# A 1x1 depthwise-separable convolution: pw loaded two thirds once and one third four times, transposes in thirds

**Chip, cores, metric.** One NeuronCore of a Trainium2 chip. The metric is the device time of one execution in microseconds (us), lower is better. Runs of a kernel are compared with runs of the kernel before on the same chip in the same rounds. A profile shows one of these executions, as the hardware profiler took it; its span is about 1.7 us shorter than the run time of the same execution.

## The reference

```python
H = W = 384; C = 384; k = 1
x: (1, H, W, C) bf16    dw: (1, 1, C) bf16    pw: (C, C) bf16
out = x * dw[0, 0]                     # k = 1: one factor for each channel
return einsum('bhwc,cd->bhwd', out, pw)
```

So out = x (147,456 rows of 384) times the matrix diag(dw) pw. x comes in and the result goes out once, 113 MB each way.

## The kernel before

x is cut into 288 supertiles of 512 rows. VectorE transposes 4-byte words, each word a pair of bf16 channels (uint32 in the profile, 876 ns for 128x384 of them). TensorE's stationary operand `T[.., par::2]` has 32 rows of channels of one parity (32*128 in the profile), and four matmuls run side by side, one in each strip of 32 array rows (`tile_position`): one takes 321 ns, yet four are done every 162.6 ns. The kernel gives each strip the scaled weights on the strip's own 32 partitions. The head of the kernel makes this fourfold, channel-sorted copy `w_r`: TensorE multiplies pw by a selection matrix `sel_w` that holds dw, and ScalarE and VectorE copy the results out of PSUM.

```python
nc.scalar.dma_start(dw_row[:], ...).then_inc(s_dw, 16)
load_x(0, nc.scalar)                                   # first x chunk: ScalarE's queue
nc.sync.dma_start(pw_n[:], pw.rearrange("(k p) d -> p k d", p=P)).then_inc(s_pw, 16)
...                                                    # then x chunks 1, 2, ... on nc.sync
w_eng = [1, 0, 1, 1, 1, 1]                             # who copies block i: 1 ScalarE, 0 VectorE
w_first = {(0, 0): [(0, 1), (1, 3)], (4, 0): [(1, 4)], (4, 1): [(1, 5)]}
...
nc.tensor.wait_ge(s_zero, 1); idle_work(3)             # 12 matmuls of zeros, in all four strips
...                                                    # dw to columns, 3 small matmuls
idle_work(3)                                           # 12 more
nc.tensor.wait_ge(s_pw, 16)
times = {(1, 1): 3, (2, 0): 2}                         # some copies repeated: 18 matmuls of 64 rows
for k in range(3): ...                                 # copies of pw to the four quadrants
with nc.tensor.Fori(0, NS // 2, 1) as it: ...          # the stream: 48 matmuls a supertile
...
for h in range(2):                                     # two transposes a supertile, 128x384 words
    ins = nc.vector.transpose(out=Tw[:, 3*h : 3*h+3], in_=Xw[:, :, j, 96*h : 96*h+96]...)
```

Of the kernel before, what the change touches and what calls it, by code (L numbers as in the profile page):

```python
# [7 lines left out]
BF16 = mybir.dt.bfloat16  # L8
F32 = mybir.dt.float32
U32 = mybir.dt.uint32  # L10
COPY = mybir.ActivationFunctionType.Copy
# [16 lines left out]
def kernel(  # L28
# [12 lines left out]
    nc = tc.nc  # L41
    P = nc.NUM_PARTITIONS
    B, H, W, C = x.shape
    assert dw.shape[0] == 1 and dw.shape[1] == 1, "only k=1 depthwise supported"
    D = pw.shape[1]
# [22 lines left out]
    pw_n = consts.tile([P, 3, D], BF16, name="pw_n")  # L68
    ones = consts.tile([P, P], BF16, name="ones")
    eye = consts.tile([P, P], BF16, name="eye")  # L70
    sel = consts.tile([P, 2, 32], F32, name="sel")
    sel_w = consts.tile([P, 3, 2, 4, 32], BF16, name="sel_w")
    w_r = consts.tile([P, NB, 2, D], BF16, name="w_r")
    dw_row = consts.tile([1, C], BF16, name="dw_row")
    dw_f = consts.tile([P, 3], F32, name="dw_f")
# [6 lines left out]
    Os = [bufp.tile([P, 4 * LMAX * D], BF16, name=f"O{i}") for i in range(NR)]  # L82
    PS = [psum.tile([P, 4, 512], F32, name=f"ps{s}") for s in range(2)]
# [3 lines left out]
    s_t = [[nc.alloc_semaphore(f"s_t{i}{h}") for h in range(2)] for i in range(2)]  # L87
# [5 lines left out]
    s_pw = nc.alloc_semaphore("s_pw")  # L93
    s_df = nc.alloc_semaphore("s_df")
    s_sw = nc.alloc_semaphore("s_sw")
    s_dwf = nc.alloc_semaphore("s_dwf")
    s_sel = nc.alloc_semaphore("s_sel")
    s_w = nc.alloc_semaphore("s_w")
    s_wr = [nc.alloc_semaphore(f"s_wr{e}") for e in range(2)]
# [3 lines left out]
    with tc.tile_critical():  # L103
# [8 lines left out]
        def load_x(t, eng=nc.sync):  # L112
            g, i, off, first, L = chunks[t]
            dst, sem, _ = x_of(t)
            rows = xf[512 * first : 512 * (first + L), :]
            if first + LONG < NS:
                src = rows.rearrange("(p s) c -> p (s c)", p=P)
                dst = dst.rearrange("p s c -> p (s c)")
                if i == 0 and g >= NR:
                    je = g_end[g - NR]  # L120
                    eng.wait_ge(s_t[je % 2][1], je // 2 + 1)
            else:
                src = rows.rearrange("(a k q) c -> q a k c", k=4, q=4)
            eng.dma_start(dst, src).then_inc(sem, 16)
# [16 lines left out]

        nc.scalar.dma_start(dw_row[:], dw.rearrange("a e c -> a (e c)")).then_inc(s_dw, 16)
        load_x(0, nc.scalar)
        nc.sync.dma_start(pw_n[:], pw.rearrange("(k p) d -> p k d", p=P)).then_inc(s_pw, 16)

# [5 lines left out]
        for _, f, t in sorted(todo, key=lambda a: a[0]):  # L151
            if f is store and t == 0:

                for _ in range(28):
                    nc.sync.wait_ge(s_pw, 16)
            f(t)
# [7 lines left out]
        w_eng = [1, 0, 1, 1, 1, 1]  # L164
        w_done = [(s_wr[e], w_eng[: i + 1].count(e)) for i, e in enumerate(w_eng)]

        w_first = {(0, 0): [(0, 1), (1, 3)], (4, 0): [(1, 4)], (4, 1): [(1, 5)]}

        def w_ps(i):
            return PS[0 if i in (2, 3) else 1][:, 2 * (i % 2) : 2 * (i % 2) + 2, :D]  # L170


        steps = [(b, par) for b in range(4) for par in range(2)] + [(4, 0), (5, 0), (4, 1), (5, 1)]

        def supertile(s, rv):
            for b, par in steps:
                for q in range(4):
                    if q == 0 and par == 0 and b in (0, 3):
                        nc.tensor.wait_ge(s_t[s][b // 3], rv)
                    if q == 0 and s == 0:  # L180
                        for e, v in w_first.get((b, par), []):
                            nc.tensor.wait_ge(s_wr[e], v)
                    mm = nc.tensor.matmul(  # L183
                        PS[s][:, q, :D],
                        lhsT=Ts[s][32 * q : 32 * q + 32, b, par::2],
                        rhs=w_r[32 * q : 32 * q + 32, b, par, :],
                        start=(b, par) == steps[0],
                        stop=(b, par) == steps[-1],
                        tile_position=(32 * q, 0),
                    )  # L190
                    if (b, par) == steps[0] and q == 0:
                        mm._wait_ge(s_a[s], rv)
                    if (b, par) in ((2, 1), (5, 1)) and q == 3:
                        mm.then_inc(s_pe)


        def idle_work(n):
            with nc.tensor.Fori(0, n, 1) as _:
                for i in range(4):
                    nc.tensor.matmul(  # L200
                        PS[0][:, i, :D],
                        lhsT=zero[32 * i : 32 * i + 32, 0:P],
                        rhs=zero[32 * i : 32 * i + 32, :],
                        start=True,
                        stop=True,
                        tile_position=(32 * i, 0),
                    )

        nc.tensor.wait_ge(s_zero, 1)
        idle_work(3)  # L210
# [3 lines left out]
        for k in range(3):  # L214
            mm = nc.tensor.matmul(  # L215
                PS[1][:, 0, D + k : D + k + 1],
                lhsT=dw_row[:, P * k : P * k + P],
                rhs=ones[0:1, 0:1],
                start=True,
                stop=True,  # L220
            )
        mm.then_inc(s_df)
        idle_work(3)
        nc.tensor.wait_ge(s_pw, 16)
        times = {(1, 1): 3, (2, 0): 2}
        for k in range(3):
            nc.tensor.wait_ge(s_sw, k + 1)
            for r in range(2):
                if k == 2:
                    nc.tensor.wait_ge(*w_done[r])  # L230

                for v in [0, 1] * times.get((k, r), 1):
                    mm = nc.tensor.matmul(  # L233
                        PS[(k + 1) % 2][:, 2 * r + v, :D],
                        lhsT=sel_w[64 * v : 64 * v + 64, k, r, :, :].rearrange("p q w -> p (q w)"),
                        rhs=pw_n[64 * v : 64 * v + 64, k, :],
                        start=True,
                        stop=True,
                        tile_position=(64 * v, 0),
                    )  # L240
                mm.then_inc(s_w)
# [5 lines left out]

        nc.gpsimd.memset(warm[:], 0.0).then_inc(s_seed)  # L248
        nc.gpsimd.memset(zero[:].bitcast(U32), 0).then_inc(s_zero)  # L249
# [9 lines left out]
        )._wait_ge(s_seed, 2).then_inc(s_sel)  # L259
        for s in range(2):  # L260
            c = nc.scalar.copy(warm[:, s + 1 : s + 2], warm[:, 0:1])  # L261
            if s == 0:
                c._wait_ge(s_seed, 1)
            c.then_inc(s_a[s])

        def transposes(t, j):
            g, i, off, first, L = chunks[t]
            jj = first + j
            s = jj % 2
            X, sem, n = x_of(t)  # L270
            Xw = X.bitcast(U32).rearrange("p (k l) c -> p k l c", l=L)
            Tw = Ts[s][:].bitcast(U32).rearrange("p b (i k) -> p b k i", k=4)
            for h in range(2):
                if h == 0 and j == 0:
                    nc.vector.wait_ge(sem, n)
                ins = nc.vector.transpose(  # L276
                    out=Tw[:, 3 * h : 3 * h + 3],
                    in_=Xw[:, :, j, 96 * h : 96 * h + 96].rearrange("p k (b w) -> p b k w", w=32),
                )
                if jj >= 2:  # L280
                    ins._wait_ge(s_pe, 2 * (jj - 2) + h + 1)
                ins.then_inc(s_t[s][h])
# [3 lines left out]
        def w_out(i):  # L286
            e, k, r = w_eng[i], i // 2, i % 2
            out, in_ = w_r[:, 2 * k : 2 * k + 2, r, :], w_ps(i)
            o = nc.vector.tensor_copy(out, in_) if e == 0 else nc.scalar.copy(out, in_)  # L289
            o._wait_ge(s_w, i + 1)  # L290
            o.then_inc(s_wr[e])
# [4 lines left out]
            in_=eye[:].rearrange("p (v w r) -> p r w v", v=2, r=2),  # L296
# [4 lines left out]
        nc.vector.tensor_copy(dw_f[:], PS[1][:, 0, D : D + 3]).then_inc(s_dwf)  # L301
        nc.vector.wait_ge(s_dwf, 2)
        for k in range(3):
            nc.vector.tensor_scalar_mul(  # L304
                sel_w[:, k], sel[:].unsqueeze(2).to_broadcast([P, 2, 4, 32]), dw_f[:, k : k + 1]
            ).then_inc(s_sw)
        for i in range(6):
            w_out(i)
# [3 lines left out]
        for jj, (t, j) in enumerate(order):  # L312
# [6 lines left out]
            if jj + 1 == NS:  # L319
                nq = 2  # L320
                nc.vector.wait_ge(s_o[g % NR], 16 * sum(map(len, groups[g % NR : g : NR])))
                e = nc.vector.tensor_copy(Ov[:, nq:4, j, :], PS[s][:, nq:4, :D])  # L322
                e._wait_ge(s_pe, 2 * jj + 2)
                e.then_inc(s_d)
            a = nc.scalar.copy(Ov[:, 0:nq, j, :], PS[s][:, 0:nq, :D])  # L325
            a._wait_ge(s_pe, 2 * jj + 2)
# [36 lines left out]
```

## Time and profile before

| | kernel before |
|---|---|
| time, 4 runs | 575.41 us (575.3 to 575.55) |
| span of the profile | 573.4 us |
| head, to the first stream matmul | 6.84 us |
| stream, 288 supertiles | 561.80 us |
| busy: TensorE, VectorE, ScalarE | 99%, 88%, 73% |

Read it as a head, a stream in which TensorE never waits, and a tail. The chain, the groups and the head in order of time are shown and read in the prediction.

The granted clock doesn't tell that TensorE runs at half clock at first: that shows in the durations of matmuls (494 ns on average for the zero matmuls of this head and up to 524 for the copies, against 321 in the stream). "Half clock" below means matmuls that long; the changed kernel's profile has four of them start to start in 320 ns, against 162.5 at full clock.

### The profile page before, as it was taken

Reading aid. Unit: us, or ns where it says so; the run is one execution under the profiler, and the core shown is the slowest. Engines: PE = TensorE matmul, PEld = TensorE weight load, DVE = VectorE, ACT = ScalarE, POOL = GpSimd, SP = SyncE. Lnnn points to the kernel's source line nnn. Section 1 sums busy time; section 2 is a strip of 40 time slices with the busy share of each in tenths; the row PEclk is TensorE's granted clock in tenths of the full one; section 3 lists DMA queues with packets and bytes.
Section 4 is the critical chain, followed back from the end, with each engine's and each line's share of the span. In section 5 each row is a group of like instructions: output and inputs, shape, how many; then the busy total and the mean of one; then the engine's idle time right before and its main releaser. Section 6 shows DMA issues by size and latency. Waiting matters only on the chain.

```text
span 573.4 us, 29717 instructions
## 1 busy us (share of the span) xinstructions
PE 566.5 (99%) x13869; PEld 414.7 (72%) x13869; DVE 506.7 (88%) x583; ACT 419.0 (73%) x296; POOL 0.9 (0%) x8
## 2 busy tenths in 40 slices
PE   8999999999999999999999999999999999999996
PEld 5777777777777777777777777777777777777774
DVE  7898889889889888988988988898898898889884
ACT  6777777777777777777777777777777777777775
POOL 0000000000000000000000000000000000000000
PEclk9999999999999999999999999999999999999999
DMA  9999999999999999999999999999999999998676
GB/s 363 420 340 434 417 425 432 445 414 422 428 414 425 387 400 427 392 408 390 430 392 385 404 425 401 396 416 421 399 392 411 418 387 393 422 401 364 267 288 233
DMA packets 25253, 226.88 MB, mean 396 GB/s; under 512 B 1178, under 2 KB 5147, under 8 KB 21403
## 3 DMA queue, kind: packets, MB, share of 16 engines
q1 hardware_dynamic: 24064, 225.61, 97.0%
q10 hardware_dynamic: 1178, 1.18, 0.6%
q14 instruction: 10, 0.07, 0.0%
q8 instruction: 1, 0.02, 0.0%
HBM read 113.54 MB, written 113.25 MB: 396 GB/s over the span
## 4 chain that ended last, share of the span: by engine, by line
PE 99%; ACT 0%; DVE 0%; issue 0%; POOL 0%; POOLq 0%; SPq 0%
PE ps L183 98%; PE ps L200 0%; ACT w_r L289 0%; DVE O L322 0%; PE ps L233 0%; POOL zero L249 0%; POOL warm L248 0%; PE ps L215 0%; POOLq L358 0%; SPq L103 0%
## 5 line engine op out<-in xcount | busy, mean ns | idle before, releaser
L183 PE MATMUL ps<-w_r,T 32*128 32x384 bf16 x13824 | 561.8, 321 | 0.7 <-ACT w_r L289 0.7
L276 DVE STREAM_TRANSPOSE T<-X 128x384 uint32<-128x384 uint32 x572 | 500.0, 876 | 56.0 <-DMA X<-in_x_dram 0.3
L325 ACT CAST O<-ps 128x1536 bf16<-128x1536 f32 x288 | 413.8, 1437 | 147.6 <-PE ps L183 147.6
L183 PEld LDWEIGHTS ps<-w_r,T 32*128 32x128 bf16 x13824 | 412.9, 93 | 149.4 <-issue 0.9
L289 ACT CAST w_r<-ps 128x768 bf16<-128x768 f32 x5 | 3.6, 818 | 1.0 <-PE ps L233 1.0
L200 PE MATMUL ps<-zero 32*128 32x384 bf16 x24 | 2.6, 494 | 1.4 <-POOL zero L249 1.4
L276 DVE STREAM_TRANSPOSE T<-Xl 128x384 uint32<-128x384 uint32 x4 | 3.5, 876 | 0.4
L322 DVE CAST O<-ps 128x768 bf16<-128x768 f32 x1 | 1.0, 958 | 3.0 <-PE ps L183 3.0
L261 ACT ACT_TABLE_LOAD x1 | 1.3, 1283 | 1.9 <-issue 1.9
L200 PEld LDWEIGHTS ps<-zero 32*128 32x128 bf16 x24 | 0.7, 99 | 2.6 <-issue 2.6
L233 PE MATMUL ps<-pw_n,sel_w 64*128 64x384 bf16 x18 | 2.2, 403 | 0.0
L233 PEld LDWEIGHTS ps<-pw_n,sel_w 64*128 64x128 bf16 x18 | 1.0, 114 | 1.3 <-issue 0.7
L294 DVE TENSOR_REDUCE sel<-eye 128x64 f32<-128x128 bf16 x1 | 0.3, 290 | 1.8 <-POOL eye L251 1.8
L289 DVE CAST w_r<-ps 128x768 bf16<-128x768 f32 x1 | 1.0, 958 | 0.9 <-PE ps L233 0.9
L304 DVE TENSOR_SCALAR sel_w<-sel,dw_f 128x256 bf16<-128x256 f32 x3 | 0.9, 350 | 0.0
L301 DVE COPY dw_f<-ps 128x3 f32<-128x3 f32 x1 | 0.2, 160 | 0.8 <-PE ps L215 0.8
L215 PEld LDWEIGHTS ps<-ones,dw_row 1*128 1x128 bf16 x3 | 0.2, 100 | 0.2 <-issue 0.2
L251 POOL TENSOR_SCALAR_AFFINE_SELECT eye<-ones 128x128 bf16<-128x128 bf16 x1 | 0.3, 292 | 0.1
L261 ACT COPY warm<-warm 128x1 f32<-128x1 f32 x2 | 0.3, 188 | 0.0
L249 POOL MEMSET zero<- 128x192 uint32 x1 | 0.3, 258 | 0.0
L215 PE MATMUL ps<-ones,dw_row 1*128 1x1 bf16 x3 | 0.2, 160 | 0.0
L250 POOL MEMSET ones<- 128x128 bf16 x1 | 0.2, 204 | 0.0
(5 smaller groups left out, 0.5 us busy)
## 6 DMA issues: line engine op xcount, KB each, us to landing
X<-in_x_dram SPq DMA_DIRECT2D x26, 3840.0 KB, 21.8
out_dram<-O SPq DMA_DIRECT2D x26, 3840.0 KB, 27.4
X<-in_x_dram SPq DMA_DIRECT2D x3, 1536.0 KB, 18.3
out_dram<-O SPq DMA_DIRECT2D x3, 1536.0 KB, 8.1
X<-in_x_dram SPq DMA_DIRECT2D x3, 768.0 KB, 7.2
out_dram<-O SPq DMA_DIRECT2D x3, 768.0 KB, 12.9
X<-in_x_dram SPq DMA_DIRECT2D x1, 2304.0 KB, 19.9
out_dram<-O SPq DMA_DIRECT2D x1, 2304.0 KB, 11.7
```

Source lines behind the costliest of these rows:

```text
L183: mm = nc.tensor.matmul(PS[s][:, q, :D], lhsT=Ts[s][32 * q : 32 * q + 32, b, par::2], rhs=w_r[32 * q : 32 * q + 32, b, par, :], start=(b, ...
L200: nc.tensor.matmul(PS[0][:, i, :D], lhsT=zero[32 * i : 32 * i + 32, 0:P], rhs=zero[32 * i : 32 * i + 32, :], start=True, stop=True, tile_p ...
L215: mm = nc.tensor.matmul(PS[1][:, 0, D + k : D + k + 1], lhsT=dw_row[:, P * k : P * k + P], rhs=ones[0:1, 0:1], start=True, stop=True,)
L233: mm = nc.tensor.matmul(PS[(k + 1) % 2][:, 2 * r + v, :D], lhsT=sel_w[64 * v : 64 * v + 64, k, r, :, :].rearrange("p q w -> p (q w)"), rhs ...
L249: nc.gpsimd.memset(zero[:].bitcast(U32), 0).then_inc(s_zero)
L251: nc.gpsimd.affine_select(out=eye[:], in_=ones[:], pattern=[[-1, P]], compare_op=mybir.AluOpType.is_equal, fill=0.0, base=0, channel_multi ...
L261: c = nc.scalar.copy(warm[:, s + 1 : s + 2], warm[:, 0:1])
L276: ins = nc.vector.transpose(out=Tw[:, 3 * h : 3 * h + 3], in_=Xw[:, :, j, 96 * h : 96 * h + 96].rearrange("p k (b w) -> p b k w", w=32),)
L289: o = nc.vector.tensor_copy(out, in_) if e == 0 else nc.scalar.copy(out, in_)
L304: nc.vector.tensor_scalar_mul(sel_w[:, k], sel[:].unsqueeze(2).to_broadcast([P, 2, 4, 32]), dw_f[:, k : k + 1]).then_inc(s_sw)
L322: e = nc.vector.tensor_copy(Ov[:, nq:4, j, :], PS[s][:, nq:4, :D])
L325: a = nc.scalar.copy(Ov[:, 0:nq, j, :], PS[s][:, 0:nq, :D])
```

## The change

The intent is a shorter head. The last two thirds of pw (rows 128 to 383, 192 KB) are loaded first and copied to the quadrants (the four groups of 32 partitions) by TensorE in four blocks instead of six. The first third is loaded directly to all four quadrants (four loads of 96 KB) and scaled there: three blocks of 128x384 by GpSimd, called its rows below, and one by ScalarE. The first x chunk moves from ScalarE's queue to second place in SyncE's. Transposes go in thirds, so that the stream can begin on the first third.

```diff
-        load_x(0, nc.scalar)
-        nc.sync.dma_start(pw_n[:], pw.rearrange("(k p) d -> p k d", p=P)).then_inc(s_pw, 16)
+        nc.sync.dma_start(w_c..., pw[C - 2 * P : C, :]...).then_inc(s_wc, 16)
+        load_x(0)
+        for q in range(4):
+            nc.sync.dma_start(w_d[32 * q : 32 * q + 32]..., pw[0 : C - 2 * P, :]...).then_inc(s_wd, 16)
...
-        idle_work(3)          # before the dw matmuls
+        idle_work(2)
...
-        idle_work(3)          # before the copies; then 18 copying matmuls of 64 rows
+        idle_work(1)          # then 8 copying matmuls of 32 rows
...
+        w_copy(2)
+        idle((2,))            # one zero matmul in one strip
+        nc.tensor.wait_ge(s_wr[1], 1)
+        w_copy(3)
+        idle((2,))
...
+        nc.gpsimd.wait_ge(s_dd, 1)
+        nc.gpsimd.wait_ge(s_wd, 64)
+        for k in (0, 1, 3):
+            nc.gpsimd.tensor_scalar(w_r[:, k // 2, k % 2, :], w_d[...], dw_d[:, k : k + 1], ...).then_inc(s_wr[2])
...
-            for h in range(2):
+            for h, (b, _) in enumerate(halves):      # three parts, 128x256 words each
```

## The prediction

> **What bounds the kernel now.** I read the chain that ended last first, because it says which part of the span a change can shorten at all. Its columns are start (us), length (us), and what ran.
>
> ```profile
> 2.85 1.18 PE ps L200 x11
> 4.02 0.45 PE ps L233 x2
> 4.47 0.02 issue
> 4.50 2.21 ACT w_r L289 x3
> 6.71 0.14 issue
> 6.84 561.80 PE ps L183 x13824
> 568.65 0.02 issue
> 568.67 0.96 DVE O L322
> ```
>
> The span of 573.4 us falls into three parts. The head lasts until the first real matmul at 6.84 us. The matmul stream lasts 561.80 us. The tail is 573.4 - 568.65 = 4.75 us (last copy out of PSUM, last store, its landing). The reader should see that in the stream TensorE hands over to no other engine. The groups of instructions, read next, confirm it:
>
> ```profile
> L183 PE MATMUL ps<-w_r,T 32*128 32x384 bf16 x13824 | 561.8, 321 | 0.7 <-ACT w_r L289 0.7
> L276 DVE STREAM_TRANSPOSE T<-X 128x384 uint32<-128x384 uint32 x572 | 500.0, 876 | 56.0 <-DMA X<-in_x_dram 0.3
> L325 ACT CAST O<-ps 128x1536 bf16<-128x1536 f32 x288 | 413.8, 1437 | 147.6 <-PE ps L183 147.6
> L289 ACT CAST w_r<-ps 128x768 bf16<-128x768 f32 x5 | 3.6, 818 | 1.0 <-PE ps L233 1.0
> ```
>
> The stream's only idle time is 0.7 us, before it starts, and it is ended by ScalarE's third copy of a weight block (L289). There are 288 supertiles of 48 matmuls: 561.80 / 288 = 1.951 us each, and 561.80 x 4 / 13824 = 0.1626 us for each four matmuls, which run side by side in four row strips.
>
> Then I read the head in order of time (start, length, engine, line, operation, count, idle before it).
>
> ```profile
> 1.02 0.43 SPq L144 DMA_DIRECT2D pw_n<-in_pw_dram  x1
> 2.63 0.21 PE L215 MATMUL ps<-ones,dw_row 1*128 1x1 bf16 x3
> 2.88 0.16 DVE L301 COPY dw_f<-ps 128x3 f32<-128x3 f32 x1 [0.76 <-PE ps L215]
> 3.08 0.88 DVE L304 TENSOR_SCALAR sel_w<-sel,dw_f 128x256 bf16<-128x256 f32 x3
> 3.96 2.22 PE L233 MATMUL ps<-pw_n,sel_w 64*128 64x384 bf16 x18
> 4.50 3.61 ACT L289 CAST w_r<-ps 128x768 bf16<-128x768 f32 x5 [0.98 <-PE ps L233]
> 4.82 0.96 DVE L289 CAST w_r<-ps 128x768 bf16<-128x768 f32 x1 [0.86 <-PE ps L233]
> ```
>
> The head is a chain: dw to columns (2.63), sel_w (first one done near 3.43), pw landed (its issue row gives 2.9 us from issue to landing, so 3.9), copying matmuls (3.96), ScalarE copies. The five ScalarE copies take 3.61 us, so one follows another every (3.61 - 0.82) / 4 = 0.70 us, and the stream waits for the third: 4.50 + 2 x 0.70 + 0.82 = 6.7.
>
> [...]
>
> **The stream after the change.** Matmuls stay 13,824 of the same shape. One more semaphore wait per supertile joins the two there were[...]. So the question is whether the transposes stay early, now 864 of 128x256 rather than 576 of 128x384. At the start, where VectorE doesn't wait for TensorE, six of them show its own pace:
>
> ```profile
> L276 DVE STREAM_TRANSPOSE T<-X x6: 846/856/858, 5.7 to 9.2; 128x384 uint32<-128x384 uint32 x6
> ```
>
> That is (9.2 - 5.7) / 5 = 0.70 us apart. If it is all proportional to size, a third takes 0.47 us; if one element costs one cycle of 1.04 ns (the 128x256 scalar multiplies above: about 267 ns apart) and 0.30 us is fixed, 0.57 us. Three cost 1.4 to 1.7 us, against 1.4 before, in a supertile of 1.95. VectorE will look nearly full, but the stream keeps 1.95 us. Change: 0.
>
> **The head, step by step.** The second part of the chain is where the change works.
> 1. dw: TensorE gets dw's row no sooner, since that DMA is issued at the same moment; two matmuls instead of three. First weights about 2.55 instead of 2.60.
> 2. dw_f copy 2.83 to 2.99. sel_w is 128x128 instead of 128x256, so the first takes about 0.22 instead of 0.35: ready at 3.25 instead of 3.43.
> 3. pw: the part that TensorE copies is 192 KB in rows of 1,536 bytes, alone at the queue's front, instead of 288 KB in 768-byte rows. I estimate landing at 3.1 to 3.4 instead of 3.9. The copying matmuls begin at 3.4 instead of 3.96: 0.55 us gained.
> 4. They are half-clock, 0.5 us: done at 3.9. ScalarE's first copy 3.95 to 4.75, while VectorE takes the second block.
> 5. Here the chain gets shorter again: the stream's first step needs two large ScalarE copies instead of three. Between them comes a 128x4 copy (starts 4.65; about 0.10 until the next may start). Second large copy 4.75 to 5.57.
> 6. 0.14 us of issue as now: the stream starts at about 5.7, against 6.84. Gain 1.1 us.
>
> Later steps of the first supertile must not stall. The block for the seventh step: fourth copying pair runs after the first copy (4.9 to 5.4), ScalarE copies it from 5.47 to 6.27, and TensorE gets there at 5.7 + 6 x 0.1625 = 6.68. GpSimd's three scaled rows start when the four direct loads have landed (about 5.1) and are needed at 7.0, 7.2 and 7.5[...].
>
> **Transfers.** The direct third comes four times, so 192 + 384 = 576 KB of pw instead of 288: 0.29 MB more, 0.7 us at 400 GB/s. Part fits into hidden gaps of the start, so x lands 0.4 to 0.7 us later. The tightest place in the trace is the first large x chunk:
>
> ```profile
> 22.67 0.88 DVE L276 STREAM_TRANSPOSE T<-X 128x384 uint32<-128x384 uint32 x1
> 23.86 3.59 DVE L276 STREAM_TRANSPOSE T<-X 128x384 uint32<-128x384 uint32 x4 [0.31 <-DMA X<-in_x_dram]
> ```
>
> Supertile 10 waits for it; TensorE needs it at 6.84 + 10 x 1.95 = 26.34, so there were 26.34 - 24.74 = 1.6 us of slack. After: landed 24.2 to 24.5, first third ready 24.9 to 25.2, needed at 5.7 + 19.5 = 25.2. The slack is just about used up, yet 3-part transposes save the 0.23 us that matter. I count 0.0 to 0.1 us.
>
> The tail moves along unchanged. Sum: -1.1 + 0.05 = about -1.0 us, or 574.4 us.
>
> **Rivals.** (a) VectorE becomes the bound. For: 576 transposes become 864, the busy share of 88% would go to nearly all. Against: the busy time of back-to-back transposes overlaps (856 ns long, 700 apart). It would need over 0.65 us from one to the next. At 0.70 it would cost 288 x 0.15 = 43 us (618). I give it 1%. (b) The gain is eaten in the first supertiles by GpSimd or the late x: at 1 us per GpSimd row the third ends at 8.1, a stall of 0.6 us, and the result is 575.0. For: nothing measures this engine here, and the tuned slack above vanishes. (c) The clock: there is less filler now (12 + 2 matmuls, in place of 24, and 8 copying matmuls, in place of 18), with TensorE idle near 4.6 and 5.5.[...] I give this 1 in 8, as two fillers look placed to prevent it. (d) pw lands no sooner[...]; then sel_w and pw still gate at 3.9 and only the shorter ScalarE chain remains, 0.6 us: 574.8.
>
> **Range and chances.** Centre 574.4. A landing at 3.1 with a fast start gives 573.9; (b), (c) in part, and (d) reach 575.4. Two per cent is 11.5 us. The whole head is 6.84 us long, so faster by 2% is impossible; slower needs (a).
>
> **What would show it.** Right: the first stream matmul at 5.5 to 6.0 us, ended by ScalarE's third copy (the second large one); stream 561.6 to 561.9 us; transposes of 128x256 under 0.75 us; tail 4.75. Wrong: idle time of the stream before GpSimd's w_r rows or before transposes that a DMA held (b), matmuls of about 500 ns after the stream starts (c), a stream of over 1.96 us per supertile (a).

That a third wait in each supertile is free was the estimate: the trace shows only that with two waits the stream's one idle time is the 0.7 us before it. That the first supertile doesn't stall on the scaled rows was not shown either.

Of the numbers:

- The 0.10 us until ScalarE may start the next copy agrees with its two 128x1 copies (188 ns each, 0.28 us for both, so 0.09 us apart).
- 1.04 ns for an element is 267 ns / 256; that it is one cycle isn't shown. The 0.22 us for the smaller sel_w is an estimate from it, 0.35 less 128 such elements.
- "Half-clock" is read from the zero matmuls of the head (494 ns, against 321 in the stream).
- The landing of pw's first part at 3.1 to 3.4 us was the author's guess. The trace gives 3.9 for the whole of pw; by size alone, 192 KB would come at 1.02 + 2.9 x 192 / 288 = 2.95. Nothing in the trace sets the value between.

## More of the kernel before

One more view is needed later: stretches of one microsecond of the kernel before, with the clock that the throttle granted, the mean busy share of the 16 DMA engines, and GB/s.

```profile
4.00:5.00 1.00, 1.00 1.04 418
5.00:6.00 1.00, 1.00 1.05 430
6.00:7.00 1.00, 1.00 1.03 412
```

In the kernel before, transfers run at 410 to 430 GB/s from 3 us on.

## The result

| | before | changed |
|---|---|---|
| time, 4 runs each | 575.41 us (575.3 to 575.55) | 576.93 us (576.49 to 577.31) |
| span of the profile | 573.4 us | 575.6 us |
| first stream matmul | 6.84 us | 6.11 us |
| first supertile ends | 8.79 us | 11.02 us |
| tail after the stream | 4.75 us | 4.73 us |

The ratio is 1.0026 (95% interval 1.0011 to 1.0040). The changed kernel is 1.5 us slower (0.26%), where 1.0 us less had been predicted, and its runs lie further apart (0.8 us against 0.25). The profiled execution is the slowest of the four.

The chain that ended last, of the changed kernel (start, length, what):

```profile
3.32 5.59 DMA O<-in_pw_dram
...
9.09 1.72 POOL w_r L306 x3
...
10.85 560.02 PE ps L194 x13780
...
570.89 0.96 DVE O L385
```

The chain of the head no longer goes through ScalarE's copies. It goes from a direct pw load that was issued at 3.32 us and took 5.59 us to land, through GpSimd's three rows, to a stream that is free of waits only from 10.85 us on. The groups:

```profile
L194 PE MATMUL ps<-w_r,T 32*128 32x384 bf16 x13824 | 563.6, 321 | 1.8 <-POOL w_r L306 1.0
L330 DVE STREAM_TRANSPOSE T<-X 128x256 uint32<-128x256 uint32 x858 | 549.6, 644 | 9.3 <-DMA X<-in_x_dram 4.4
L306 POOL TENSOR_SCALAR w_r<-O,dw_d 128x384 bf16<-128x384 bf16 x3 | 1.7, 581 | 6.1 <-DMA O<-in_pw_dram 6.1
```

GpSimd sat idle for 6.1 us until the direct loads came; its rows themselves take 0.58 us each. The head in order of time (start, length, ...):

```profile
3.83 0.80 ACT L344 CAST w_r<-ps 128x768 bf16<-128x768 f32 x1 [0.73 <-PE ps L229]
...
5.37 1.55 DVE L330 STREAM_TRANSPOSE T<-X 128x256 uint32<-128x256 uint32 x3 [0.54 <-DMA X<-in_x_dram]
...
6.11 2.75 PE L194 MATMUL ps<-w_r,T 32*128 32x384 bf16 x32 [0.61 <-ACT w_r L344]
9.01 0.61 ACT L369 ACTIVATE w_r<-O,dw_d 128x384 bf16<-128x384 bf16 x1 [2.90 <-DMA O<-in_pw_dram]
...
9.82 10.47 PE L194 MATMUL ps<-w_r,T 32*128 32x384 bf16 x240 [0.96 <-POOL w_r L306]
```

ScalarE's first copy starts 0.67 us sooner than before (3.83 against 4.50), and the stream 0.73 us sooner. What ends the wait before the stream is not the copy that its line names: its first step needs ScalarE's second large copy, which ended at 5.40 us, and the first third of the transposes, which ended at 6.01, since x's first chunk landed only at 5.35. (The copy that ended at 6.10 is the third large one, for the seventh step.) The first 32 matmuls take 2.75 us; at full clock it would be about 1.5 (seven steps of 0.1625 and a last matmul of 0.32). The durations of these 32 (minimum, median, maximum in ns) say why:

```profile
L194 PE MATMUL ps<-w_r,T x32: 475/522/523, 6.1 to 8.3; 32*128 32x384 bf16 x32
```

They ran at half clock: start to start, a group of four took 320 ns instead of 162.5. In all, the first supertile took 11.02 - 6.11 = 4.91 us instead of 1.95. Its 2.96 us of loss is 1.2 us of slow matmuls and 1.75 us of waiting for GpSimd's rows, and from the second supertile on every group takes 162.5 ns again. The balance of the profile is -0.73 + 2.96 = +2.23 us, which is the difference of the spans (575.6 - 573.4). The two losses overlap: at full clock TensorE would have reached the first GpSimd row at 7.41 us and waited for it until 9.82 all the same. So in this profile the late rows alone decide when the first supertile ends.

The transfers, in the same stretches as before:

```profile
4.00:5.00 1.00, 1.00 0.74 183
5.00:6.00 1.00, 1.00 1.02 278
6.00:7.00 1.00, 1.00 0.91 355
```

For three microseconds they move 183 to 355 GB/s instead of 412 to 430. In the trace each load has 16 steps of its semaphore. Of the 64 steps of the direct loads 62 had come by 6.56 us, the last two only at 8.53 and 8.91; of the 16 of the second x chunk, 15 by 7.42 and the last at 9.66. I read that as one of the sixteen DMA engines two microseconds behind the others, on top of a slump of all; the records don't name the engine, so it isn't shown.

### The profile page after: what moved, and what is told of

Its sections match the earlier page's. It is cut to its first block, busy times and chain, and to the rows that moved or that the text cites. A ratio compares the mean times of both kernels' runs of the same rounds, so it can differ in the third digit from the quotient of the medians.

```text
span 575.6 us, 30118 instructions
## 1 busy us (share of the span) xinstructions
PE 566.7 (98%) x13852; PEld 356.8 (62%) x13852; DVE 556.6 (97%) x871; ACT 418.0 (73%) x296; POOL 3.0 (1%) x11
## 4 chain that ended last, share of the span: by engine, by line
PE 97%; DMA 1%; SPq 0%; POOL 0%; DVE 0%; issue 0%; POOLq 0%
PE ps L194 97%; DMA O<-in_pw_dram 1%; POOL w_r L306 0%; SPq L155 0%; DVE O L385 0%; SPq L131 0%; SPq L150 0%; SPq L421 0%; POOLq L304 0%; SPq L110 0%
## 5 line engine op out<-in xcount | busy, mean ns | idle before, releaser
L330 DVE STREAM_TRANSPOSE T<-X 128x256 uint32<-128x256 uint32 x858 | 549.6, 644 | 9.3 <-DMA X<-in_x_dram 4.4
L194 PEld LDWEIGHTS ps<-w_r,T 32*128 32x128 bf16 x13824 | 355.8, 93 | 209.8 <-issue 2.9
L330 DVE STREAM_TRANSPOSE T<-Xl 128x256 uint32<-128x256 uint32 x6 | 3.9, 644 | 0.0
L344 ACT CAST w_r<-ps 128x768 bf16<-128x768 f32 x3 | 2.3, 816 | 0.7 <-PE ps L229 0.7
L229 PE MATMUL ps<-O,sel_w 32*128 32x384 bf16 x8 | 1.3, 498 | 0.9 <-ACT w_r L344 0.6
L306 POOL TENSOR_SCALAR w_r<-O,dw_d 128x384 bf16<-128x384 bf16 x3 | 1.7, 581 | 6.1 <-DMA O<-in_pw_dram 6.1
```

Of the source, the lines that this page charges most:

```text
L194: mm = nc.tensor.matmul(PS[s][:, q, :D], lhsT=Ts[s][32 * q : 32 * q + 32, b, par::2], rhs=w_r[32 * q : 32 * q + 32, b, par, :], start=n == ...
L229: mm = nc.tensor.matmul(ps[:, at + u - u0, :D], lhsT=sel_w[32 * u : 32 * u + 32, par, :, :].rearrange("p q w -> p (q w)"), rhs=w_c[32 * u ...
L306: nc.gpsimd.tensor_scalar(w_r[:, k // 2, k % 2, :], w_d[:, k // 2, k % 2, :], dw_d[:, k : k + 1], 1.0, mybir.AluOpType.mult, mybir.AluOpTy ...
L330: ins = nc.vector.transpose(out=Tw[:, b : b + 2], in_=Xw[:, :, j, 32 * b : 32 * b + 64].rearrange("p k (b w) -> p b k w", w=32),)
L344: o = nc.vector.tensor_copy(out, in_) if e == 0 else nc.scalar.copy(out, in_)
```

## The experiments

Times are medians; "before" is the kernel before in the same rounds. The clock is read from the trace's own record of it, which has a time from which the full clock (1.0) was granted.

| run | time, us | before, us | ratio, 95% interval | full clock from, us |
|---|---|---|---|---|
| again | 576.52 | 575.44 | 1.0019 (1.0002 to 1.0036) | 8.80 |
| thirds_only | 575.34 | 575.44 | 1.0005 (0.9989 to 1.0022) | 5.47 |
| wd_128x1 | 576.19 | 575.44 | 1.0008 (0.9991 to 1.0025) | 11.44 |
| wd_128x4 | 576.45 | 575.44 | 1.0018 (1.0001 to 1.0035) | 10.34 |
| x0_second | 575.45 | 575.47 | 1.0000 (0.9983 to 1.0017) | 6.93 |
| x0_second_b | 575.42 | 575.52 | 0.9998 (0.9978 to 1.0018) | 6.28 |
| dead_loads | 575.76 | 575.47 | 1.0007 (0.9990 to 1.0024) | 5.54 |
| x0_on_act | 577.50 | 575.47 | 1.0039 (1.0022 to 1.0056) | 12.23 |
| wd_128x4_act | 576.33 | 575.52 | 1.0015 (0.9998 to 1.0032) | 8.86 |
| fill | 576.46 | 575.47 | 1.0019 (1.0002 to 1.0036) | 9.19 |
| act_fill | 577.30 | 575.52 | 1.0033 (1.0016 to 1.0050) | 11.63 |
| act_fill_row | 576.46 | 575.52 | 1.0017 (1.0001 to 1.0034) | 9.75 |
| wide | 576.62 | 575.52 | 1.0025 (1.0012 to 1.0037) | 7.09 |
| late_issue | 576.82 | 575.52 | 1.0033 (1.0018 to 1.0047) | 9.03 |
| late_wide | 576.44 | 575.52 | 1.0014 (1.0001 to 1.0027) | 7.54 |
| before_thin | 577.16 | 575.52 | 1.0035 (1.0020 to 1.0049) | 10.33 |
| split_pw | 578.00 | 575.33 | 1.0036 (1.0023 to 1.0049) | 12.18 |
| act_wide_row | 576.99 | 575.33 | 1.0035 (1.0023 to 1.0047) | 8.47 |

In the profiles of the kernel before and the changed one the full clock came at 5.19 and 9.07 us.

### Does it repeat? (again)

No edit.

> The changed kernel once more, unedited, to see whether what its first profile shows repeats: the last of the direct pw loads landing at 8.9 us although 62 of its 64 semaphore steps were there at 6.6, the second x chunk landing at 9.7 with 15 of 16 steps at 7.4, and the first 32 stream matmuls at about 520 ns. Theory P (the loads to 32 partitions each are what holds a DMA engine up): it repeats, last landing over 7.5 us, time 576.4 to 577.4. Theory C (one engine was late by chance in that run): last landing 6.5 us or below in this profile, and times spread over 575.8 to 577.3.

The last direct load landed at 7.32 us this time, the second x chunk at 8.32, without one single late engine but with a slump just as long (about 200 GB/s from 4.5 to 6 us). Neither theory had its number. The first eight groups were again at 320 ns. So the slump and the late clock repeat; the single late engine doesn't. The loss lies elsewhere in part: the first supertile lost 1.7 us (1.4 to the half clock, 0.3 to GpSimd's rows), and before the third supertile TensorE waited 0.88 us longer than a group takes, for transposes of the third x chunk (landed at 11.42 us, against 7.81 in the kernel before). From its chain:

```profile
11.55 0.71 issue
12.26 557.90 PE ps L194 x13728
```

With the earlier start these sum to -1.08 + 1.7 + 0.9 = +1.5 us, the difference of the spans (574.9 - 573.4). The runs went from 575.61 to 577.59.

### The transposes alone (thirds_only)

```diff
 # in the kernel before
-            for h in range(2):
+            for h in range(3):
-                    out=Tw[:, 3 * h : 3 * h + 3],
-                    in_=Xw[:, :, j, 96 * h : 96 * h + 96]...
+                    out=Tw[:, 2 * h : 2 * h + 2],
+                    in_=Xw[:, :, j, 64 * h : 64 * h + 64]...
 # and three waits and signals a supertile instead of two
```

> The kernel before with nothing but the transposes and their waits in thirds (128x256, three waits and three signals per supertile). My prediction: the stream stays at 1.950 us a supertile and the time at 575.4, within 0.2. Rival (VectorE, busy 97% in the changed kernel, has become a bound or adds a wait somewhere): over 575.9.

The stream is as it was, to the tenth of a microsecond:

```profile
L183 PE MATMUL ps<-w_r,T 32*128 32x384 bf16 x13824 | 561.8, 321 | 0.5 <-ACT w_r L289 0.5
L276 DVE STREAM_TRANSPOSE T<-X 128x256 uint32<-128x256 uint32 x858 | 549.8, 643 | 6.0 <-DMA X<-in_x_dram 0.5
```

VectorE is busy for 549.8 us instead of 500.0 and TensorE doesn't notice. Back to back, the thirds start 0.47 us apart (three in 1.4 us), which is two thirds of the 0.70 us of the larger ones. The part of the change that touches the stream costs nothing.

### The shape of the direct loads (wd_128x1, wd_128x4)

Both give a wrong result: as many bytes, but read from rows of x, so that a load can fill 128 partitions. So they also test whether it matters that four loads read the same 96 KB of pw.

```diff
-        for q in range(4): ...  # 32 partitions each
+        nc.sync.dma_start(w_d (128 partitions), xf[0:512, :].rearrange("(b p t) d -> p b (t d)", b=2, t=2))   # wd_128x1
+        for b, r in ...: nc.sync.dma_start(w_d[:, b, r, :], 128 rows of xf)                                 # wd_128x4
```

> Wrong result on purpose: the direct third is loaded by one DMA to all 128 partitions, same bytes and same 1536-byte pieces, but other data (rows of x[...]). Theory P (shape of 32 partitions): landing by 5.5 us, second x chunk by 6.5, no stall before GpSimd's rows; [...]the first supertile ends at about 9.2 instead of 11.0 and the time is 575.4 + 0.4 = 575.8. Theory Q (four issues of 0.47 us each in SyncE's queue): the same, 575.8, as the issues are gone as well. Theory C or a landing that is late for another reason: no change, 576.9.

> Wrong result on purpose: four DMAs as in the changed kernel, same bytes each, but each to all 128 partitions (768 bytes to each, rows of x). Theory P: landing by about 6.0 us, all 64 steps within 1 us of each other, 575.8 to 576.0. Theory Q (the four issues, not the shape): as the changed kernel, landing near 8.9, 576.9.

The one load landed at 8.13 us, the four at 7.05. With one issue in place of four the slump was still there, and with all partitions too (200 to 329 GB/s in the halves of a microsecond from 4 to 6.5 us in wd_128x1, 172 to 292 in wd_128x4). Neither the 32-partition shape nor the number of issues, nor reading pw four times, is the cause by itself. In both runs the clock came very late (11.44 and 10.34 us), and in wd_128x1 the stream ran at half clock until 11.4 us.

### The queue alone, and the loads alone (x0_second, x0_second_b, dead_loads)

```diff
 # x0_second: in the kernel before
-        load_x(0, nc.scalar)
         nc.sync.dma_start(pw_n[:], ...).then_inc(s_pw, 16)
+        load_x(0)
 # dead_loads: in the kernel before, with load_x(0, nc.scalar) kept
         nc.sync.dma_start(pw_n[:], ...).then_inc(s_pw, 16)
+        for q in range(4): ...  # the changed kernel's direct loads, into a buffer that is free until supertile 20
```

> The kernel before with only the first x chunk moved from ScalarE's queue to second place in SyncE's. Theory R (what slows the transfers of the head in all changed kernels is that everything is in one queue): the rate between 4 and 9 us falls from 415 to 200 to 350 GB/s as there, the second x chunk's steps spread over more than 1 us, time up by 0.3 or more. Rival (one queue is harmless): 400 GB/s and more from 3.5 us on, spread below 0.6 us, 575.4.

> The kernel before with the first x chunk second in SyncE's queue, once more, for a second profile: if one queue is the cause of the slump, 180 to 310 GB/s at 5 to 6.5 us and a spread of the second x chunk's steps over 1 us come again; if they were chance, 400 GB/s and a spread below 0.6 us.

> The kernel before, x's first chunk still in ScalarE's queue, plus the four direct loads to 32 partitions each right after pw; nothing in the head uses or waits for them. Theory D (the four loads themselves slow the transfers): rate 150 to 350 GB/s for some microseconds after 4 us, second x chunk from 5.85 to 8 us or later, but its use is at 8.2 at the earliest, so the time is 575.4 to 576.2. Theory R (one queue): 400 GB/s and more, second x chunk at 6.9 (four issues of 0.47 us later at most), 575.4.

x0_second, from its stretches (the same columns):

```profile
5.00:6.00 1.00, 1.00 1.16 267
6.00:7.00 1.00, 1.00 0.68 230
```

dead_loads:

```profile
5.00:6.00 1.00, 1.00 1.14 261
6.00:7.00 1.00, 1.00 1.01 290
```

Either part of the change alone brings a slump into the kernel before, and x0_second did so in both of its profiles (215, 147 and 160 GB/s in the halves from 5.0, 5.5 and 6.0 us in the second). They look different: in x0_second DMA engines are idle for part of the time (0.68), with dead_loads they are busy and slow (1.01 and more). The packet records of the kept traces fit this. In the kernel before, a packet of 3,072 bytes takes 121 ns at the median, and between 4 and 7 us 2 of 289 packets take over twice the usual time of their size. In x0_second it is 18 of 216, with 35% of all packet time (the longest takes 1.81 us); in dead_loads nearly all are slower, at the median 1.37 times the usual. The time hardly suffers (575.45 and 575.76 against 575.47). In the profiles the stream starts 0.25 to 0.4 us later than in the kernel before, as pw lands 0.2 to 0.3 us later and x0_second's copies run longer at half clock (the clock came at 6.93 and 6.28); the second x chunk is then in time in all three. dead_loads shows the tight place that the prediction named: its stream stops for 0.34 us before supertile 10, where the first large x chunk is late (landed at 25.9 us instead of 23.8).

### The first x chunk back, with and without the shape (x0_on_act, wd_128x4_act)

```diff
 # x0_on_act: in the changed kernel
-        load_x(0)
+        load_x(0, nc.scalar)
 # wd_128x4_act: this and the four 128-partition loads (wrong result on purpose)
```

> The changed kernel with the first x chunk back in ScalarE's queue. Theory R: direct loads land by 5.5, second x chunk by 6.5; the clock still lifts late, so the first supertile ends near 9.3 and the time is 575.9. Theory D: landing of the direct loads at 6.5 to 9 as in the changed kernel, 576.3 to 577.

> Wrong result on purpose: the changed kernel with the first x chunk in ScalarE's queue and four direct loads of the same bytes to all 128 partitions each (rows of x). Theory of two separate causes (one queue for all leaves DMA engines idle; loads to 32 partitions keep them busy but slow): with both taken away 400 GB/s and more from 3.5 us on, no slump, direct loads landed by 5.3, second x chunk by 6.6. Rival (any small loads at this place slow the head): 250 to 300 GB/s between 4.5 and 6.5 as with the first chunk on ScalarE's queue alone. Time depends on the clock: 575.5 to 577.5.

With the chunk on ScalarE's queue no single engine was far behind: the direct loads were complete at 6.64 us and the second x chunk within 7.05 to 7.56. But both kernels still had a slump (264 and 310 GB/s between 5 and 6 us, 344 and 237 between 6 and 7). So the theory of two separate causes fell too: with both removed, 310 and less remained. x0_on_act is the slowest of this group because of the clock. Its stream never waits for a row; it starts at 6.29 us and runs the whole first supertile and half of the second at half speed.

### Filler for the clock, in one strip (fill, act_fill, act_fill_row)

```diff
 # fill: in the changed kernel
-        idle_work(1)
+        idle(range(4)); idle(range(4))
-        idle((2,))                       # twice
+        idle((2,) * 3)                   # twice
 # act_fill: this, x0 on ScalarE's queue, idle_work(3) at the start
 # act_fill_row: this, and VectorE scales one of GpSimd's rows
```

> The changed kernel with more zero matmuls: eight instead of four before the pw copies, three instead of one in each of the two gaps after them, so that TensorE has no gap over 0.2 us from 1.45 us to the stream. Theory of the clock[...]: from about 5.5 us all matmuls take about 321 ns. The direct loads still arrive at 7.3 to 8.9, so TensorE then only waits for GpSimd's rows: time 576.2 to 576.9, up to 0.4 less than the changed kernel. Rival[...]: matmuls of 520 ns past 8 us as before.

> The changed kernel with the first x chunk in ScalarE's queue and with zero matmuls in all of TensorE's gaps (three rounds of four at the start instead of two, eight before the pw copies, three in each later gap). Theory of the clock[...]: it comes at 4.9 to 8.3 us instead of 12.2, the first supertile then waits for GpSimd's third row at most; 575.3 to 576.2, that is 1.3 to 2 us less than without the filler. Rival (filler in one row strip doesn't count): clock at 9 us or later, 576.5 and more.

> As act_fill, and VectorE scales one of GpSimd's three rows, so that GpSimd has two. If GpSimd's third row (to 8.5 us) is what holds the first supertile once the clock is up: 0.3 to 0.5 us less than act_fill, 574.9 to 575.6, level with the kernel before or a little better. If the clock or the second x chunk holds it: no difference to act_fill.

My theory was that TensorE's gaps hold the full clock off (0.32, 0.57 and 0.61 us of them before the stream in the first profile of the changed kernel). The clock came no sooner (9.19, 11.63, 9.75 us, against 9.07 and 8.80), although TensorE was never idle from 1.45 to 6.36 us in act_fill_row. So the theory fell. What the profiles then showed goes with the rows of the array that the matmuls use (each record has its number of active rows). I took the 3.4 us before the full clock came and the 3.4 us before those, a length that I set and that no run shows, and added up the time in which matmuls stream (320 ns each at half clock, 160 at full), weighted with the array rows that they use out of 128:

```
                 last 3.4 us before the clock came    the 3.4 us before those
before                     0.84                             0.09
dead_loads                 0.79                             0.18
x0_second                  0.92                             0.47
after                      0.75                             0.33
again                      0.88                             0.39
fill                       0.94                             0.47
act_fill                   1.00                             0.58
act_fill_row               0.90                             0.44
x0_on_act                  1.00                             0.77
```

In all 20 profiles the stretch before the clock came has 0.75 or more at this length, and the one before that 0.77 or less. Other lengths keep the order in the first profiles of both kernels: with 3.0 us it is 0.85 after 0.21 in the kernel before and 0.85 after 0.27 in the changed one, with 3.8 us 0.84 after 0.00 and 0.68 after 0.46. act_fill_row's 0.44 is a stretch without any gap. Whether there is a line at all and where, over which length, and why 0.77 once did not do, stays open. The kernel before has dense copies of 64 rows and twelve more zero matmuls in all strips; the changed kernel has 0.33 to 0.39 in the earlier stretch.

act_fill_row also took GpSimd's third row away, and its time is 0.8 us under act_fill's. The profiles tell which of the two did it: in neither does the stream wait for a row. It lost 2.41 us in act_fill and 1.47 in act_fill_row, all of it in groups at half clock, so the clock, 1.9 us sooner, made the difference there.

### Filler with all rows, and its converse (wide, before_thin)

```diff
 # wide: in the changed kernel
+        def idle_all(n):
+            for _ in range(n):
+                nc.tensor.matmul(PS[0][:, 2, :D], lhsT=zero[:, 0:P], rhs=zero[:, :], start=True, stop=True)
-        idle_work(1)
+        idle_all(2)
-        idle((2,))                       # after w_copy(2) and after w_copy(3)
+        idle_all(2)                      # and idle_all(3)
 # before_thin: in the kernel before
-        idle_work(3)                     # the second one
-        times = {(1, 1): 3, (2, 0): 2}
+        times = {}
```

> The changed kernel with filler that is 128 rows deep (zero matmuls over all four row strips, two before the pw copies, two and three in the gaps after them) in place of the one-strip filler. Theory of the clock by occupied rows[...]: it comes between 5 and 8.3 us instead of 8.8 to 9.1. The first supertile then waits for GpSimd's rows only, ends at 9.2 to 9.6 or later as the direct loads land: 576.0 to 576.6, 0.2 to 0.6 below the changed kernel. Rival (rows don't matter): clock at 8.8 or later, no change.

> The kernel before without its second filler (12 zero matmuls) and without the repeated copying matmuls: the converse. Theory of the clock: it comes at 8.5 to 10.3 instead of 5.2, after the stream's start at 6.85, so the first supertile or two run half speed for 1.7 to 3.4 us: 0.8 to 1.7 us more, 576.2 to 577.2, with runs more than 0.5 us apart. Rival (the clock is not what costs the changed kernel): 575.4.

The converse is clear: with twelve zero matmuls and six repeated copies gone, the kernel before gets the clock at 10.33 us instead of 5.19 and is 1.6 us slower. Its chain ends in

```profile
7.03 563.41 PE ps L183 x12095
```

which is 1.61 us more stream than 561.80, all of it in ten and a half groups at 320 ns. (The stream also starts 0.19 us later, for x's first chunk.) wide got the clock at 7.09 us, two groups after the stream's start. That this is the filler's doing fits the table above (0.78, of which zero matmuls are 0.47, so that zeros count as well), and late_wide repeats it (7.54 us, 0.82). The time, though, is only 0.3 us under the changed kernel's first measurement and no better than again's. The rest went into the transfers. TensorE and VectorE in wide:

```profile
6.48 4.87 PE L194 MATMUL ps<-w_r,T 32*128 32x384 bf16 x96
11.85 0.66 PE L194 MATMUL ps<-w_r,T 32*128 32x384 bf16 x10 [0.51 <-issue]
```

```profile
11.12 1.57 DVE L334 STREAM_TRANSPOSE T<-X 128x256 uint32<-128x256 uint32 x3 [1.66 <-DMA X<-in_x_dram]
```

The first supertile lost 0.5 us to GpSimd's rows (direct loads at 7.11 us). Before the third one, at 11.85 us, TensorE had to wait 0.68 us longer than a group takes for the transposes that start at 11.12, since the third x chunk landed at 11.02 us instead of 7.81. again, with its late clock, lost 0.88 us at the same place; so repairing the clock leaves this loss about as it was.

### Holding back the large loads (late_issue, late_wide)

```diff
+            if f is load_x and t == 3:
+                nc.sync.wait_ge(s_wd, 64)        # late_issue; late_wide has idle_all as well
```

> The changed kernel, but SyncE issues the large x chunks (the fourth on) only when the direct pw loads have landed. In all profiles the slump of the transfer rate ends within about a microsecond of SyncE's last issue of the head, and the two kernels without a slump have their issues out by 4.4 us. Theory I (issuing, or the many descriptors that wait in the queue, is what slows the transfers): with them held back the direct loads land by 5.8, the second x chunk by 6.6, no slump over 0.7 us; the clock still costs about 1 us: 575.6 to 576.2. Theory of the small loads themselves: direct loads land at 6.5 to 9 as before, 576.5 to 577.5.

> Both edits. If both theories hold, the stream starts at 5.8 to 6.1, at full clock for most of the first supertile, and GpSimd's third row is ready by 7.7: first supertile ended at 8.0 to 8.5 against 8.8 in the kernel before, time 574.7 to 575.2, better than both kernels. If only the clock theory holds: as wide. If only Theory I: as late_issue.

With nothing but pw and the first three x chunks in the queues, late_issue still moved 301 and 200 GB/s from 4 to 5 and 5 to 6 us, and the direct loads landed at 7.58 us. So it isn't the backlog of large loads, and Theory I as I stated it fell. late_wide came out as wide did (576.44 us, where 574.7 to 575.2 was expected if both theories held). Holding the loads back costs something later: its stream stops again at 27 us, for 0.6 us.

### Two attempts at a better kernel (split_pw, act_wide_row)

```diff
 # split_pw: in the kernel before
-        nc.sync.dma_start(pw_n[:], ...)
+        nc.sync.dma_start(pw_n[:, 0, :], pw[0:P, :]).then_inc(s_pw, 16)
+        nc.sync.dma_start(pw_n[:, 1:3, :], ...).then_inc(s_pw2, 16)
-        idle_work(3)
+        idle_work(2)
 # act_wide_row: the changed kernel with x0 on ScalarE's queue, idle_all, one row on VectorE
```

> The kernel before, with what worked in the changed kernel and nothing that didn't: pw once, in two loads, the first 128 rows ahead, so that the copies can begin before all of pw is there; one filler round less, so that it doesn't stand in their way; the first x chunk stays in ScalarE's queue and no direct loads. If the early part of pw is what gave the changed kernel its earlier start: first copy out of PSUM at 3.9 to 4.1 instead of 4.5, stream from 6.3 to 6.5, clock still before 8.3, time 574.9 to 575.3. Rival (any further load in the head brings the slump and delays x): stream stalls on x, 575.4 or more.

> The changed kernel repaired as far as the runs so far tell how: 128-row filler, the first x chunk in ScalarE's queue, VectorE scaling one of GpSimd's rows. Clock before 8.3; GpSimd's second row ready by 8.4 as direct loads land at 6.6 to 7.1; the first supertile ends at 8.6 to 9.0; second x chunk at 7.6 to 7.9: 575.4 to 576.0, 0.5 to 1.2 less than the changed kernel, at best level with the kernel before. If it is still over 576.3, a third cause is at work (x landing late for the later supertiles).

split_pw is the slowest kernel, and shows a late load and a late clock once more without any of the changed kernel's code:

```profile
1.46 4.43 DMA pw_n<-in_pw_dram
5.89 0.14 issue
6.02 2.42 PE ps L237 x14
8.44 0.02 issue
8.46 563.61 PE ps L185 x13085
```

The second pw load, 192 KB issued at 1.46 us, took 4.43 us to land, where the kernel before had all 288 KB in 2.9 us. The slump is another here: 229 GB/s from 3 to 4 us (before: 410), and 384 to 392 from 4 to 7. TensorE was idle from 4.40 to 6.02 us, and the clock came only at 12.18 us; one filler round had gone as well, and the run doesn't separate the two. In act_wide_row the profiled stream starts at 6.73 us and never waits; it lost only 0.85 us to the clock (8.47 us). That run took 575.81 us, but its runs go up to 578.60, and the median (576.99) is over the 576.3 above which a further cause was expected; no slow run of it has a profile, so that stays open. No version beat the kernel before clear of noise.

## Why the prediction was wrong

**Right.** The stream didn't change: 162.5 ns for four matmuls from the second supertile on, and thirds_only shows that the third wait and the smaller transposes cost nothing. Rival (a) is out. The transposes are 0.47 us apart, the lower of the two values I had worked out. The tail (4.73; 4.75) is as said. GpSimd's rows took 0.58 us each and ScalarE's row 0.61. pw's first part landed at 3.25 us (3.1 to 3.4 predicted), so rival (d) is out too. The start of the stream was 6.11 us in the first profile, outside the predicted 5.5 to 6.0, and 5.77 in the second. Its cause was not as said: step 6 had it wait for ScalarE's second large copy (5.57; measured 5.40 and 5.58), but what came last in both was the first third of the transposes (6.01 and 5.67), held by x's first chunk, which landed at 5.35 and 5.00. The prediction never timed this chunk, so that 5.77 lies near 5.7 is in part luck.

**Wrong: "GpSimd's three scaled rows start when the four direct loads have landed (about 5.1)".** They landed at 8.91, 7.32 and, with x on the other queue, 6.64 us. I had taken 0.29 MB more at 400 GB/s, and so a shift of x by 0.4 to 0.7 us. What happened is not more bytes at the old rate but a lower rate for all, 183 to 355 GB/s for three microseconds, so that the second x chunk came at 9.66 instead of 5.85 us. (Behind the direct loads it was also issued 2.3 us later, at 3.79 instead of 1.51, which the prediction left out; but wd_128x1 issued it at 2.38 and it still landed at 9.12.) The part of the transfers was the term of the sum that failed: I had 0.05 us for it, and in the first profile the wait for GpSimd's rows alone is 1.75 us, in the second it is 0.3 and that for the third x chunk 0.9. Rival (b) had this wait and 575.0 us for it, from GpSimd rows of 1 us; they took 0.58, and their data came late.

**Wrong: the clock.** Rival (c) named it, but I gave it 1 in 8, because two fillers looked placed to prevent it, and its own sum lay above the end of my range. It came true in both profiles of the changed kernel: full clock at 9.07 and 8.80 us, 1.2 and 1.4 us lost. I counted matmuls (14 and 8 for 24 and 18) but not the array rows that they use. Taking filler and repeats from the kernel before costs it 1.6 us by itself, as much as the changed kernel's whole loss (1.5, and 1.1 in again).

**What stays open.** Why the transfers slow down is not settled. These runs exclude as the only cause: chance (the slump is in every profile of the changed kernel and its variants), the 32-partition shape, the number of issues, one queue for all, and the backlog of large loads. The packet records exclude one more, the size of the pieces: in the changed kernel packets of 1,536 bytes take 65 ns at the median and those of 3,072 bytes 121, so the small ones are about as fast for each byte; but between 4 and 7 us 27 of 360 packets take over twice the usual time. Moving the first x chunk alone and adding the loads alone each bring a slump, and splitting the pw load an earlier one. Nor do the medians tell the share of clock and transfers: in the two profiles both cost over a microsecond, and repairing the clock alone (wide) gained 0.3 us on the first measurement and nothing on again.

## What to carry to other kernels

Here a short head was worth less than what the longer one kept up: without twelve zero matmuls and six repeated copies (before_thin) the full clock came at 10.33 us instead of 5.19, and the kernel was 1.6 us slower. So before cutting filler or repeated matmuls, count how much of the array they occupy, rows included, until the full clock has come. Adding up bytes at the rate of the steady stream (400 GB/s) did not tell when small loads land in the first microseconds: the direct loads were expected at about 5.1 us and were all there at 8.91 and 7.32. Put a measured landing into the sum, or keep what such loads feed off the path. Where the stream has no idle time, as here, a gain of one microsecond in the head has to survive run-to-run effects of the same size (575.61 to 577.59 us in again).
